# A long convolution by FFT with a maxout MLP behind it: the spectral stage in 32x64 and 64x32 tiles, with the complex product made whole

## The chip, the cores and the metric

The kernel runs on one core of a Trainium2 chip. The metric is the device time of one execution in microseconds, lower is better. Three executions of the kernel before took 496.3, 496.51 and 496.91 us; the median is 496.51. Engines go by the names of the profile: PE is TensorE (matmuls), PEld its weight loads, DVE VectorE, ACT ScalarE, POOL GpSimd, SP SyncE, which only issues DMAs.

## The reference

```python
# x (8, 3072, 256), filt_r and filt_i (1537, 256), all float32
X = np.fft.rfft(x, axis=1)
Y = X * (filt_r + 1j * filt_i)[None]
y = np.fft.irfft(Y, n=3072, axis=1)
# the 8*3072 rows of y as tokens; w1, w2 (256, 1024), w_out (1024, 256)
out = np.maximum(y @ w1, y @ w2) @ w_out          # (24576, 256) float32
```

Each of eight batches is filtered along its 3072 positions in the frequency domain, and every position then goes through a two-branch maxout MLP.

## The kernel before

**The MLP.** Since max(a, b) = max(a - b, 0) + b, the kernel computes relu(y (w1 - w2)) w_out + y (w2 w_out). Wd is w1 - w2, Wo is w_out, and M is w2 w_out, made once. A batch's 3072 tokens are eight tiles of 384. For a tile tt, `moe_h` makes eight hidden blocks: ph, 128 hidden units by 384 tokens, is two matmuls (L483), and is evicted through a relu into gt by DVE (L485) or ACT (L487). `moe_o` of tile tt - 1 runs between them: each block of 128 tokens takes ten matmuls of 256 columns into po (two with M, L535, eight with Wo, L537); two blocks share a bank, DVE evicts them to ot (L548), and `out_block` issues the output DMAs (L496), on POOL's queue for all but the last two tiles.

**The step grid.** The order of the work is written out by hand. The last loop of the kernel goes over tiles tt and j = 0 to 7; a batch is 64 steps, step = 8 (tt mod 8) + j. One step is ph of (tt, j), then three or four po matmuls of tile tt - 1. The FFT of the coming batches is slipped into steps: the table `mid` holds calls made right behind ph, ahead of the po matmuls; `group` holds `s4g` calls made behind the first two po matmuls; `todo` (filled by `plan`) holds calls at a step's end. Each engine takes its instructions in this program order.

**The filter** of a batch has four matmul stages; n runs over parts of the 24 frequency groups, s and g over halves.

- The load and fold: `load_xf` brings a quarter of a half batch from memory (SP), `fold` adds and subtracts the two halves of the sequence on POOL (L104, L105) into xb, in bf16. c = 0 to 7 are the eight quads of a batch.
- S1, `s1`: a quad is four matmuls of 512 columns into two banks, pa0 and pa1, in 64x64 tiles (64 rows of contraction, 64 output columns; four of them cover the 128x128 array). ACT evicts them to `at` (L359), SP writes `ad` in DRAM, and `s1_read` brings it back with the axes turned, as bt.
- S2, `s2`: eight 64x64 matmuls of 256 columns into px0 and px1 (L385). For a frequency group they give the real and the imaginary part of X in different rows.
- The product, `product` on DVE (L391): px times the filter F, both parts of the filter at once, 1024 elements a row, to bf16 pq. It makes the partial products only: X_r F_r, X_r F_i, X_i F_r, X_i F_i.
- S3, `s3`: 16 matmuls of 64x64 and 256 columns into pz0 and pz1 (L409), with the tables VP and VQ. They take the partial products and so do the sums of the complex product in the contraction, along with the first step of the inverse transform. ACT evicts to zt (L413), SP writes `zd` in DRAM, and `z_read` brings it back as zr.
- S4, `s4g`: 16 matmuls of 48 rows for each tile (L444) into pc0, pc1, then ACT (L449) and two DVE operations (L451) give the tokens y of two or three tiles.

`visit(b, n, quads)` puts S3 of part n - 1, S2 of part n, S1 of the listed quads of the batch after it, and the product of part n behind one ph. There are seven visits in a batch, n = 0 to 6, called right behind ph (`mid`), at steps 14, 18, 23, 31, 34 (or 35), 39 and 47 in the batches 2 and later of the grid, a step or so later in batch 1. `s4g` stands at steps 61 (of the batch before), 6 and 27. Batch 0, and the filter of batch 1 within it, go by code of their own (`s1t`, `t1`, `s3t`, `t2`, `f1`, `s4`).

**PSUM.** The pool `ps` has six banks, one for each of ph, pa0, pa1, px0, px1, pz0, pz1, pc and so on; `pso` has two, for po. A tile gets the bank whose last tile was given back first, and its first matmul waits for the engine that reads that one.

ACT_TOO (L475) lists steps at which ACT takes a relu that DVE would take otherwise: from batch 1 on, DVE has 19 of a batch's 64 relus.

## Time and profile before

| | |
|---|---|
| median of three executions | 496.51 us |
| the profiled execution: its own time, and its span | 496.87 us, 495.1 us |
| mean granted clock of TensorE | 0.993 of full speed |
| time between the s4g calls at step 61 of two batches (212.56 to 269.23) | 56.67 us |
| matmuls and weight loads, by the page | 5759 each |
| DMA queue of SP: packets, MB | 64178, 66.71 |
| DMA queue of POOL: packets, MB | 13200, 29.60 |
| HBM read, written | 53.87 MB, 47.19 MB |

The profiled execution is one run under the hardware profiler; the span goes from its first instruction to its last. The page gives busy time by engine, the chain of work that ended last, and the costliest groups of instructions with the idle time ahead of them and what ended it. The views of the trace used below are tables of busy time in chosen stretches, the waits of an engine with what ended them, single lines of the kernel with their durations, and the timeline: start, length, engine, line, operation, what is written from what, how many in a row. Matmuls overlap: one starts before the end of the one ahead of it, so the time of a matmul is read from start to start.

### The profile page before, as it was taken

The numbers are of one execution on the slowest core, as the hardware profiler recorded it, in microseconds if no ns is written. First come the engines' busy times: TensorE is split into PE (matmuls) and PEld (weight loads), VectorE is DVE, ScalarE is ACT, GpSimd is POOL, SyncE is SP. The second block draws the span as 40 slices with busy tenths as digits, with TensorE's granted clock in tenths as the row PEclk, the third lists the DMA queues.
The fourth block names the chain that finished last, engine by engine and source line by source line (L and its number), as shares of the span: only waits on it lengthen the run. The fifth ranks groups of instructions, "written<-read, shape, count | busy, mean of one in ns | idle before, by whom it ended". The sixth has DMA issues, their size and how long they took to land.

```text
span 495.1 us, 14211 instructions
## 1 busy us (share of the span) xinstructions
PE 483.3 (98%) x5759; PEld 353.0 (71%) x5759; DVE 335.5 (68%) x535; ACT 320.3 (65%) x667; POOL 259.7 (52%) x342
## 2 busy tenths in 40 slices
PE   7689999999999999999999999999999999999997
PEld 3457777777777777777777777777777777777775
DVE  7786788467855788458865688458874688556542
ACT  5776478666765677566866677666766656465442
POOL 8795869436368574556637575475642212222220
PEclk9889999999999999999999999999999999999999
DMA  7989998995899786896888966895777435531112
GB/s 120 163 241 229 264 243 258 279 254 167 232 264 250 175 240 194 259 241 186 214 250 234 228 200 201 267 251 166 214 228 190 127 124 152 155 122 66 64 65 86
DMA packets 77587, 97.31 MB, mean 197 GB/s; under 512 B 8945, under 2 KB 55314, under 8 KB 76146
## 3 DMA queue, kind: packets, MB, share of 16 engines
q1 hardware_dynamic: 64178, 66.71, 50.0%
q0 software_dynamic: 13200, 29.60, 21.6%
q8 instruction: 45, 0.74, 0.7%
q14 instruction: 20, 0.16, 0.1%
q10 hardware_dynamic: 144, 0.09, 0.1%
HBM read 53.87 MB, written 47.19 MB: 204 GB/s over the span
## 4 chain that ended last, share of the span: by engine, by line
PE 94%; ACT 2%; DMA 2%; POOL 1%; issue 0%; DVE 0%; POOLq 0%
PE po L537 35%; PE ph L483 34%; PE po L535 9%; PE pz L409 5%; PE pc L444 3%; PE pa L355 2%; PE px L385 2%; DMA xb<-in_x_dram 2%; PE pr L609 1%; PE pt L588 1%; POOL xb L89 1%; PE pa L330 1%; PE py L461 1%; PE pt L582 0%; ACT bt L574 0%
## 5 line engine op out<-in xcount | busy, mean ns | idle before, releaser
L487 ACT ACTIVATE gt<-ph 128x384 bf16<-128x384 f32 x357 | 175.6, 496 | 137.6 <-PE ph L483 134.5
L537 PE MATMUL po<-Wo,gt 128*128 128x256 bf16 x1528 | 262.6, 273 | 0.0
L496 POOL DMA_DIRECT2D out_dram<-ot x186 | 102.9, 556 | 195.5 <-DVE ot L548 179.9
L537 PEld LDWEIGHTS <-gt 128*128 128x128 bf16 x1528 | 144.7, 98 | 66.7 <-issue 12.0
L391 DVE TENSOR_TENSOR pq<-px,F 128x1024 bf16<-128x1024 f32 x91 | 106.9, 1218 | 26.4 <-PE px L385 25.4
L485 DVE TENSOR_SCALAR gt<-ph 128x384 bf16<-128x384 f32 x155 | 83.7, 551 | 52.2 <-PE ph L483 45.9
L483 PEld LDWEIGHTS <-Wd 128*128 128x128 bf16 x1024 | 99.4, 98 | 14.0 <-POOL Wd L298 0.7
L548 DVE TENSOR_SCALAR ot<-po 128x512 f32<-128x512 f32 x83 | 57.0, 686 | 35.0 <-PE po L537 33.1
L104 POOL TENSOR_TENSOR xb<-XF 128x512 bf16<-128x512 f32 x48 | 61.3, 1276 | 23.6 <-DMA XF<-in_x_dram 10.4
L105 POOL TENSOR_TENSOR xb<-XF 128x512 bf16<-128x512 f32 x48 | 61.1, 1272 | 0.0
L359 ACT ACTIVATE at<-pa 128x512 bf16<-128x512 f32 x96 | 51.8, 613 | 3.4 <-PE pa L355 3.3
L413 ACT ACTIVATE zt<-pz 128x512 bf16<-128x512 f32 x84 | 45.6, 594 | 5.7 <-PE pz L409 1.9
L449 ACT ACTIVATE ce<-pc 128x384 f32<-128x384 f32 x56 | 23.7, 491 | 6.3 <-PE pc L444 5.5
L409 PE MATMUL pz<-pq,VP 64*64 64x256 bf16 x336 | 22.2, 281 | 0.0
L385 PE MATMUL px<-bt,U 64*64 64x256 bf16 x384 | 20.2, 280 | 1.2 <-ACT VQ L279 0.7
L409 PE MATMUL pz<-pq,VQ 64*64 64x256 bf16 x336 | 21.1, 269 | 0.0
L409 PEld LDWEIGHTS <-VP 64*64 64x64 bf16 x336 | 10.0, 105 | 13.3 <-issue 12.7
L355 PE MATMUL pa<-xb,CT 64*64 64x512 bf16 x192 | 18.0, 377 | 0.0
L444 PEld LDWEIGHTS <-zr 48*128 48x128 bf16 x896 | 12.9, 93 | 4.4 <-issue 4.4
L444 PE MATMUL pc<-G,zr 48*128 48x48 bf16 x896 | 15.1, 180 | 0.0
L385 PEld LDWEIGHTS <-U 64*64 64x64 bf16 x384 | 10.6, 108 | 3.9 <-issue 3.6
L619 PE MATMUL pd<-W 128*128 128x512 bf16 x28 | 9.6, 456 | 1.5 <-DVE zero L150 1.5
(383 smaller groups left out, 632.0 us busy)
## 6 DMA issues: line engine op xcount, KB each, us to landing
out_dram<-ot POOLq DMA_DIRECT2D x186, 128.0 KB, 3.7
XF<-in_x_dram SPq DMA_DIRECT2D x96, 192.0 KB
ad<-at SPq DMA_DIRECT2D x56, 192.0 KB
zd<-zt SPq DMA_DIRECT2D x42, 256.0 KB
zr<-zd SPq DMA_DIRECT2D x56, 192.0 KB
bt<-ad SPq DMA_DIRECT2D x72, 128.0 KB
WS<-in_moe_w_dram SPq DMA_DIRECT2D x4, 512.0 KB
xb<-in_x_dram POOLq DMA_DIRECT2D x8, 192.0 KB, 6.6
```

The source lines that it names most:

```text
L104: G.tensor_tensor(t_[:, 0], f[:, 0], f[:, 1], OP.add)
L105: G.tensor_tensor(t_[:, 1], f[:, 0], f[:, 1], OP.subtract)
L359: S.activation(at[:, m0:m0 + 2], pa[g], AF.Copy)
L391: E.tensor_tensor(pq, px.rearrange("p (o i) d -> p o i d", o=1).to_broadcast([128, 2, 2, D]), F[:, :, 2 * v:2 * v + 2, s], OP.mult)
L409: TE.matmul(pz[g][64 * s:64 * s + 64, i], tab[64 * g:64 * g + 64, 2 * v + i, s], pq[s][64 * g:64 * g + 64, q, i], start=(q == 0), stop=(q ...
L413: S.activation(zt[:, :, g], pz[g], AF.Copy)
L483: TE.matmul(ph, Wd[:, dc, 128 * j:128 * j + 128], y_[:, dc], start=(dc == 0), stop=(dc == 1))
L485: V.tensor_scalar(gt[tt][:, j], ph, 0.0, None, OP.max)
L487: S.activation(gt[tt][:, j], ph, AF.Relu)
L496: E.dma_start(out=dst, in_=ot[tt // 2][:, 3 * (tt % 2) + c])
L537: TE.matmul(p_, g_[:, n - 2, blk], Wo[:, n - 2], start=(e == 0), stop=(e == 9))
L548: V.tensor_scalar(ot[tt // 2][:, e - 1:e + 1], po[q // 2 % 2], SCALE, None, OP.mult)
```

## The change

The filter of batches 2 to 7 goes another way; batch 0 and batch 1 keep theirs.

1. **S2 in pairs, 64x32 tiles** (`s2_pairs`): sixteen matmuls for eight. The rows of px now hold, for four frequency groups of 32 rows, the real part in one half of the columns and the imaginary part in the other. It needs a table UN, a negative copy of a part of U.
2. **The complex product whole.** `product_pairs` makes the four partial products of n = 0 to 4 on DVE in fp32, as before 1024 elements a row (a small extra operation at n = 0 for one frequency); three steps later `add_pairs` subtracts and adds them on POOL, four operations of 256 elements a row, into one bf16 tile ri. For n = 5 `whole_product` does all of it on DVE: for each half s two multiplications of 512 elements a row, one of them in place in PSUM, and two sums of 256.
3. **S3 once, 32x64 tiles** (`s3_pairs`): 32 matmuls of 32 rows for two parts n at once, into four banks pz0 to pz3, where before the two parts took 32 matmuls of 64 rows. The evictions stay four for two parts; at the third of the three calls of a batch DVE takes two of them.
4. **S1 in 64x32 tiles** for batches 3 and later: eight matmuls of 512 columns a quad for four.
5. **A new plan.** `group_of` puts S3, then the first quad of S1, then S2 and its product, then the other quads behind the first two po matmuls of a step, where `s4g` stands too. Groups at steps 9, 14, 20, 30, 34, 38, 44; `s4g` at 61, 4 and 25. The z reads come in thirds (`z_read3`); loads, folds and the `s1_read` calls have new steps.
6. **Tables.** `to_pairs`, at steps 54, 56 and 60 of batch 0: the copies for UN, fN, VQ, and four DMAs inside F that bring the filter into the order of pairs.
7. **Other places.** From tile 8 on every second output DMA goes by SP's queue. VS gives the steps at which DVE takes the relu: again 19 of 64, in the last batch 24. pqpool has four buffers for six, pq0 eight for six, and w2b and w2T lie in the pool of the fp32 products (`pfpool`, three buffers).

The core of the diff, with the new functions (whole, but for the lists of pools):

```diff
+        if b == 2:
             for g, r in ((0, 0), (1, 1), (0, 1), (1, 0)):
                 TE.matmul(pa[g][64 * r:64 * r + 64], CT[64 * g:64 * g + 64, r], xb[b, c][64 * g:64 * g + 64, r], ...)
+        else:
+            for r in range(2):
+                for h in range(2):
+                    for g in range(2):
+                        TE.matmul(pa[g][64 * r + 32 * h:64 * r + 32 * h + 32], CT[64 * g:64 * g + 64, r, 32 * h:32 * h + 32],
+                                  xb[b, c][64 * g:64 * g + 64, r], start=True, stop=True)
...
+    def s2_pairs(b, n):
+        px = [ps.tile([128, 2, D], FP32, tag="ps", name="px%d" % s) for s in range(2)]
+        for k in range(2):
+            for q in range(4):
+                g, r = divmod(q, 2)
+                u = 4 * n + 2 * r + g
+                for s in range(2):
+                    rows = slice(64 * s, 64 * s + 64)
+                    tab = U[rows, u, 32 * (k ^ r):32 * (k ^ r) + 32] if k * r == 0 else UN[rows, n, g]
+                    TE.matmul(px[s][32 * q:32 * q + 32, k], tab, bt[b][rows, u], start=True, stop=True)
+        return px
+    def filt(n, s, c):
+        return F[:, c, 2 * n, s].rearrange("p (o d) -> p o d", o=1).to_broadcast([128, 2, D])
+    def product_pairs(n, px):
+        pf = []
+        for s in range(2):
+            t_ = pfpool.tile([128, 2, 2, D], FP32, tag="pf", name="pf")
+            V.tensor_tensor(t_, px[s].rearrange("p (o k) d -> p o k d", o=1).to_broadcast([128, 2, 2, D]),
+                            F[:, :, 2 * n, s].rearrange("p c (o d) -> p c o d", o=1).to_broadcast([128, 2, 2, D]),
+                            OP.mult)
+            if n == 0 and s == 0:
+                V.tensor_tensor(t_[0:1, 0, 1], px[0][0:1, 1], fN, OP.mult)
+            pf.append(t_)
+        return pf
+    def whole_product(n, px):
+        ri = pqpool.tile([128, 2, 2, D], BF16, tag="pq", name="ri")
+        for s in range(2):
+            t_ = pfpool.tile([128, 2, D], FP32, tag="pf", name="pf")
+            V.tensor_tensor(t_, px[s], filt(n, s, 1), OP.mult)
+            V.tensor_tensor(px[s], px[s], filt(n, s, 0), OP.mult)
+            V.tensor_tensor(ri[:, s, 0], px[s][:, 0], t_[:, 1], OP.subtract)
+            V.tensor_tensor(ri[:, s, 1], px[s][:, 1], t_[:, 0], OP.add)
+        return ri
+    def add_pairs(b, n):
+        ri = pqpool.tile([128, 2, 2, D], BF16, tag="pq", name="ri")
+        for s, t_ in enumerate(pend[b, n]):
+            G.tensor_tensor(ri[:, s, 0], t_[:, 0, 0], t_[:, 1, 1], OP.subtract)
+            G.tensor_tensor(ri[:, s, 1], t_[:, 0, 1], t_[:, 1, 0], OP.add)
+        pend[b, n] = ri
+    def s3_pairs(b, k, ris):
+        if k == 0:
+            zd[b] = dram.tile([NU, 128, D], BF16, tag="zd", name="zd")
+        pz = [ps.tile([128, 2, D], FP32, tag="ps", name="pz%d" % q) for q in range(4)]
+        for i in range(2):
+            for c, tab in enumerate((VP, VQ)):
+                for s in range(2):
+                    for q in range(4):
+                        rows = slice(32 * q, 32 * q + 32)
+                        TE.matmul(pz[q][64 * s:64 * s + 64, i], tab[rows, 4 * k + 2 * i + q % 2, s],
+                                  ris[i][rows, s, c], start=(c == 0), stop=(c == 1))
+        for g in range(2):
+            zt = zpool.tile([128, 2, 2, D], BF16, tag="zt", name="zt")
+            for r in range(2):
+                if k == 2 and g == 1:
+                    V.tensor_copy(zt[:, :, r], pz[2 * g + r])
+                else:
+                    S.activation(zt[:, :, r], pz[2 * g + r], AF.Copy)
+            nc.sync.dma_start(out=zd[b][8 * k:8 * k + 8].rearrange("(i r g) p d -> g p i r d", r=2, g=2)[g], in_=zt)
+    def group_of(b, n, k, quads):
+        if k is not None:
+            s3_pairs(b, k, [pend.pop((b, 2 * k + i)) for i in range(2)])
+        if b + 1 >= B:
+            quads = ()
+        for c in quads[0:1]:
+            s1(b + 1, c)
+        if n is not None:
+            px = s2_pairs(b, n)
+            pend[b, n] = whole_product(n, px) if n == 5 else product_pairs(n, px)
+        for c in quads[1:]:
+            s1(b + 1, c)
...
-    ACT_TOO = ((7, 6), (0, 1), (0, 6), (1, 1), (3, 6))
+    VS = (1, 3, 8, 13, 18, 24, 28, 30, 34, 38, 44, 46, 48, 50, 52, 54, 56, 58, 60)
...
-        E = G if tt < 8 * B - 2 else nc.sync
+        E = G if tt < 8 or (tt < 8 * B - 2 and (3 * tt + c) % 2 == 0) else nc.sync
...
     for b in range(1, B - 1):
+        for st, n, k, quads in ((9, 0, None, (0, 1)), (14, 1, None, (2, 3)), (20, 2, None, (4,)), (30, 3, 0, ()),
+                                (34, 4, None, (5, 6)), (38, 5, 1, ()), (44, None, 2, (7,))):
+            groups[b, st] = (b + 1, n, k, quads)
+            if n is not None and n < 5:
+                plan(b, st + 3, add_pairs, b + 1, n)
+        for k, n in enumerate((37, 46, 48)):
+            plan(b, n, z_read3, b + 1, k)
...
+            elif (b, step) in groups:
+                moe_o(tt - 1, k, k + 2)
+                group_of(*groups[b, step])
+                k, n = k + 2, n - 2
```

## What was predicted

> **What bounds the kernel now.** I read the page first (busy time, then the chain that ended last), then a table of busy time over a whole batch, then PE's own waits, then the timeline around one visit.
>
> ```profile
> span 495.1 us, 14211 instructions
> ...
> PE 483.3 (98%) x5759; PEld 353.0 (71%) x5759; DVE 335.5 (68%) x535; ACT 320.3 (65%) x667; POOL 259.7 (52%) x342
> ...
> PE 94%; ACT 2%; DMA 2%; POOL 1%; issue 0%; DVE 0%; POOLq 0%
> ```
>
> ```profile
> 269.23:325.90 56.67, 56.67 (x674) 41.73 (x674) 38.95 (x60) 38.72 (x82) 33.21 (x41) 1.00 0.83 225
> ```
>
> ```profile
> PE pa L559 <- DMA xb<-in_x_dram: 1.8, 3, 1.3
> ```
>
> The columns of the table are length, PE, PEld, DVE, ACT, POOL, granted clock and DMA share. A batch takes 56.67 us, PE is busy in all of it at full clock, and the waits put down to PE (ten kinds, this the largest, under 8 us in all) lie in the opening stages. So time goes only where PE streams, changes tile shape, or waits less than the tail of a matmul, which "busy" hides. DVE has 18 us free in a batch, ACT 18, POOL 23.
>
> One visit of before (S3, S2, S1 between a ph and the next ph):
>
> ```profile
> 306.89 0.49 PE L483 MATMUL ph<-y__5618,Wd 128*128 128x384 bf16 x2
> 307.31 0.30 PE L409 MATMUL pz<-pq,VP 64*64 64x256 bf16 x4
> 307.44 0.28 PE L409 MATMUL pz<-pq,VQ 64*64 64x256 bf16 x4
> 307.55 0.28 PE L409 MATMUL pz<-pq,VP 64*64 64x256 bf16 x4
> 307.66 0.28 PE L409 MATMUL pz<-pq,VQ 64*64 64x256 bf16 x4
> 307.77 0.39 PE L385 MATMUL px<-bt,U 64*64 64x256 bf16 x8
> 307.99 0.39 PE L355 MATMUL pa<-xb,CT 64*64 64x512 bf16 x4
> 308.30 0.50 PE L537 MATMUL po<-Wo,gt 128*128 128x256 bf16 x3
> 308.68 0.48 PE L483 MATMUL ph<-y__5623,Wd 128*128 128x384 bf16 x2
> 309.00 0.38 PE L535 MATMUL po<-M,y__5618 128*128 128x256 bf16 x2
> 309.22 0.38 PE L537 MATMUL po<-Wo,gt 128*128 128x256 bf16 x2
> 309.44 0.49 PE L483 MATMUL ph<-y__5623,Wd 128*128 128x384 bf16 x2
> ```
>
> ```profile
> 308.03 1.08 ACT L413 ACTIVATE zt<-pz 128x512 bf16<-128x512 f32 x2
> ```
>
> Four 64x64 matmuls of 256 columns run as one round: rounds start 0.11 us apart, 0.13 behind the entry. A visit's S3 is 4 rounds, S2 two, an S1 quad (512 columns) one of 0.22. The two matmuls of a ph stream 0.325 us (a step of ph and four po takes 0.76, from 308.68 to 309.44, and a po of 256 columns 0.109 like a round), so ph ends at 307.21 and the first S3 round starts 0.09 later. From the S1 round at 307.99, 0.22 long, to po at 308.30 is again 0.09. These are the prices of a change of shape.
>
> ```profile
> 226.13 0.49 PE L483 MATMUL ph<-y__4375,Wd 128*128 128x384 bf16 x2
> ...
> 227.56 0.33 PE L483 MATMUL ph<-y__4375,Wd 128*128 128x384 bf16 x1
> ```
>
> From one ph to the next, less 0.325 for ph and 0.109 for each po, that first visit of a batch (S2, S1) costs 0.67 us; the one above 1.79 - 0.325 - 0.327 = 1.14. All seven visits from 226 to 259 us, worked the same way: 0.67, 1.10, 1.10, 1.10, 1.12, 1.14, 1.14, together **7.37 us**. In the last producing batch, without S1, it is 0.45, five of 0.89 and 0.67, together 5.55.
>
> **What the change removes and adds on PE.** S3 goes from 24 rounds in a batch to 12, if eight 32x64 tiles run in a round: 12 x 0.109 = 1.31 us less. S2 and S1 double their instructions (16 and 8 for 8 and 4) in tiles half as wide, the same rounds if eight run at once. No 32-row tile is in the trace; 64x32 is, at the building of the tables:
>
> ```profile
> 20.75:20.79 0.04, 0.03 (x8) 0.03 (x8) 0.04 (x1) 0.04 (x1) 0.04 (x1) 1.00 0.11 15
> 20.79:20.82 0.03, 0.03 (x16) 0.03 (x16) 0.03 (x1) 0.03 (x1) 0.03 (x1) 1.00 0.04 0
> ```
>
> In stretches of 0.032 us the count of matmuls under way grows by 8: eight 64x32 tiles start every 32 ns, so eight in 109 ns is no limit of issue. I take full concurrency for 32x64 too (nearest row); the other end is four at a time. The Trainium skill, "TensorE: Matmul & The Clock Gate", section "Wait — 56ns, not 53.3ns?", says start-to-start never drops below about 25 ns; by that, 18 S3 groups of 32 matmuls would take 0.80 us for 0.44 and 36 S2 of 16 take 0.40 for 0.22, 13 us more and 509 in all. The rows above show 4 ns from start to start, so by them the rule does not hold for tiles side by side, and I give it no chance beyond that of the last rival.
>
> Shape changes: seven entries and exits stay; three groups of a batch now change inside from 32x64 to 64x32, which no row shows; between nothing and the 0.13 us of an entry's first round plus 0.09, I take 0.09 plus 0.02 of slower first round. If nothing else happened, a middle batch's seven groups would cost three at 1.03 (S3 with S2 or S1), three at 0.89 (S1, S2, S1) and one at 0.69: 6.5 us, 0.9 less than 7.37.
>
> **What then is late.** ps has six banks. A group of six takes them all, and in the built program the next ph gets the bank that the group's first tile held (pz0, or pa0). Its eviction must end first. The chain in before:
>
> ```profile
> 400.29 0.28 PE L409 MATMUL pz<-pq,VQ 64*64 64x256 bf16 x4
> ...
> 400.61 1.09 ACT L413 ACTIVATE zt<-pz 128x512 bf16<-128x512 f32 x2
> ```
>
> ```profile
> 170.13 0.39 PE L355 MATMUL pa<-xb,CT 64*64 64x512 bf16 x4
> ...
> 170.56 0.60 ACT L359 ACTIVATE at<-pa 128x512 bf16<-128x512 f32 x1 [0.84 <-PE pa L355]
> ```
>
> ```profile
> L413 ACT ACTIVATE zt<-pz 128x512 bf16<-128x512 f32 x84 | 45.6, 594 | 5.7 <-PE pz L409 1.9
> ```
>
> From the start of the last S3 round, 0.32 us to ACT, 0.594 for pz0, and 0.05 to PE (308.03 + 0.594 = 308.62, ph at 308.68): 0.97. In before S2, S1, the exit and three po cover it to within 0.04 us, which is the difference between 1.10 and 1.14 above. In the changed kernel two of the four po stand ahead of the group and S3 and S1 are seldom together, so less stands behind S3:
>
> - Groups at steps 30, 38 (S3, S2) and 44 (S3, S1). ph ends at 0; two po 0.218, change 0.094, rounds at 0.31, 0.45, 0.555, 0.664. pz0's last matmul is the fifth of eight, with a wait on a weight load ahead of it: 0.03 to 0.04 more. Next ph at 0.664 + 0.04 + 0.97 = 1.67. PE alone would be there at about 1.47. Less four po: **1.235** each instead of 1.03.
> - Groups at 9, 14, 34 (S1, S2, S1). pa0 starts at 0.31, its last matmul 0.04 later; 0.43 to ACT, 0.605, 0.05: next ph at 1.44, PE alone 1.32. Less four po: **1.00** each.
> - Group at 20 has four tiles: no wait, 0.69.
>
> Sum 3.71 + 3.00 + 0.69 = 7.40, against 7.37: +0.03 us a batch, five times. The dearer the inner change of shape, the more of it these waits hide, up to 0.2 us. In the last producing batch there is no S1: four groups at 0.45, two at 1.235, one S3 alone 0.71, sum 4.98 against 5.55: -0.57. **Together 0.15 - 0.57 = -0.4 us**.
>
> The Trainium skill, "TensorEngine Tiling (Array Packing)", section "PSUM Bottleneck", speaks against the change in the same sense: after a speedup by tiling the PSUM copy may become the bottleneck. By that sentence alone all 0.9 us a batch could go; the rows above say how much of it does.
>
> **Work beside PE, costed at nothing.**
>
> ```profile
> L496 POOL DMA_DIRECT2D out_dram<-ot x186 | 102.9, 556 | 195.5 <-DVE ot L548 179.9
> ...
> L391 DVE TENSOR_TENSOR pq<-px,F 128x1024 bf16<-128x1024 f32 x91 | 106.9, 1218 | 26.4 <-PE px L385 25.4
> ...
> L548 DVE TENSOR_SCALAR ot<-po 128x512 f32<-128x512 f32 x83 | 57.0, 686 | 35.0 <-PE po L537 33.1
> ```
>
> ```profile
> L399 POOL TENSOR_TENSOR pq<-xs,F x1: 660/660/660, 32.8 to 32.8; 128x256 bf16<-128x256 f32 x1
> ```
>
> ```profile
> L397 DVE TENSOR_TENSOR pq<-px,F x1: 680/680/680, 32.9 to 32.9; 128x512 bf16<-128x512 f32 x1
> ```
>
> ```profile
> L398 DVE TENSOR_TENSOR pq<-px,F x1: 411/411/411, 33.5 to 33.5; 128x256 bf16<-128x256 f32 x1
> ```
>
> POOL: an add_pairs is four 128x256 operations, 4 x 0.66 = 2.64 us, five in a batch, 13.2; half of the output DMAs leave it (12 x 0.55 = 6.6). 33.2 + 6.6 = 40 of 56.7. In order behind folds, the add of product 3 ends some 5 us after the ph of step 30 (the product 3.7, then half an add), and the S3 of step 38 comes 8.4 after it (1.35 for the rest of group 30, the group at 34, seven steps of 0.65 or 0.76): 3 us of cover, beyond which PE waits for POOL one to one. DVE: ten products of 1.22 (fp32 out is in no row of that shape, but the 128x512 fp32 eviction and the bf16 product differ by 0.01), one small extra (0.41), a whole product and two zt copies (0.68): 38.95 + 3.7 = 42.6. The whole product at step 38 is four operations of 0.68 and four of 0.41, overlapping by 0.08, 4.0 us; it starts 1.36 after ph and ends at 5.4, and S3 of step 44 needs its second half at 6.1: 0.65 us of cover. ACT loses two evictions. SP gains 12 output DMAs and four reads a batch and waits in order for DVE's evictions; behind them stand x loads, used eleven steps later, and the z reads, needed 13 steps (9.5 us) after step 48. The table steps at 54 to 60 are a few small operations and four DMAs, ten steps ahead of use.
>
> **The sum.** The profiled run took 496.87 (span 495.1, 1.8 around it): 496.87 - 0.4 = 496.45. It stands 0.36 above the median of 496.51; on the median's footing **496.1 us**. Differences under 0.2% (1 us: 495.5 to 497.5) are about what a measurement of this kernel cannot tell from no change.
>
> **Rivals.**
>
> 1. The eviction does not hold the next ph. For: the stalls are 0.1 to 0.2 us each, inside a matmul's tail, and the tiles may drain sooner. Against: 1.14-us visits show exactly this wait. Then 0.9 us a batch is won five times, and 1.0 in the last (two groups at 1.03 for 1.235): 5.5 us, 491. Half of it gives 493.5. Chance 0.28 for 491 to 495.
> 2. DVE becomes late at step 44. Beyond 0.65 us of delay, each us holds S3 on PE, in six batches. The in-place multiplications in PSUM and the self-waits of the whole product are in no row. If the two in-place ones take twice 0.68, DVE ends 1.36 later, PE waits 0.7, 4.3 us in all: **500.4**. For: four dependent operations in a row, with an eviction and a relu right behind. Against: DVE stays idle a quarter of the batch. Chance 0.22 for 497.5 to 501.
> 3. The change does not do what it says: 32-row tiles run four at a time. Then each of 18 S3 groups has 0.436 more: 496.1 + 7.8 = 504. Against: the 64x32 rows. Chance 0.08.
>
> The forecast, that waits behind the new groups take back what S3 gives, has 0.42, with its own range 494.8 to 497.5. Of it I put 0.30 within 0.2%, 0.08 below, 0.04 above. So faster 0.28 + 0.08 = 0.36, same 0.30, slower 0.22 + 0.08 + 0.04 = 0.34. The range takes rival 1 to 493.0 and rival 2 to 500.5; outside stay about 0.07 below and 0.11 above.
>
> **What the new profile would show.** Right: S3 rounds of eight starting 0.11 us apart, four to a group; a change inside the group of about 0.1; the ph behind steps 30, 38, 44 starting 0.05 us after the first zt ends, about 1.67 after the ph before; a middle batch of 56.7 us, the last shorter by 0.5. Wrong: PE waiting for POOL or DVE at S3 (rival 2), S3 rounds 0.22 apart (rival 3), or a ph right behind two po with zt still running (rival 1).

## The result: 515.7 us after 496.7, and the profile after the change

The changed kernel took 515.73 us in the median of four runs (514.75 to 517.65), the kernel before 496.71 (496.30 to 497.78) beside it: a ratio of 1.0384, 95% interval 1.035 to 1.0419. It is 19 us slower, outside the range on record. The profiled execution took 517.65 us.

The page of the kernel after: the span, the busy times, the granted clock in 40 slices, the chain that ended last.

```profile
span 515.8 us, 15430 instructions
...
PE 489.7 (95%) x6204; PEld 347.1 (67%) x6207; DVE 359.5 (70%) x597; ACT 308.5 (60%) x651; POOL 297.7 (58%) x381
...
PEclk9889999999998999989999899999999999999999
...
PE 73%; DMA 8%; SPq 5%; issue 4%; POOL 4%; ACT 3%; DVE 1%; POOLq 0%; ACTq 0%; DVEq 0%
PE ph L591 27%; PE po L645 26%; PE po L643 7%; DMA zr<-zd 5%; PE pc L552 3%; SPq L387 3%; PE pa L365 2%; PE pz L501 2%; DMA xb<-in_x_dram 2%; SPq L97 1%; ACT zt L509 1%; PE px L457 1%; POOL xb L107 1%; DMA XF<-in_x_dram 1%; SPq L372 1%
```

PE had 94% of the chain before and has 73 now, and the granted clock shows eights where all was full speed behind the opening. The largest part of what took its place is the z read (zr<-zd): its transfers have 5%, and SP's issue of them at L387 has 3%. The waits of PE and of its weight loads say where it is felt (total us, times, longest):

```profile
PE pc L552 <- DMA zr<-zd: 9.4, 9, 2.4
```

```profile
PEld L552 <- DMA zr<-zd: 6.1, 4, 2.7
```

L552 is `s4g`. Its cost at step 61, worked out like the visits of the prediction (ph to ph, less 0.325 and 0.109 for each po), was 0.83 us before; in four batches it is now 4.07, 4.56, 3.43 and 2.97 us. From 95 us to the last s4g, the s4g calls cost 30.5 us for 16.2, steps without a call 6.1 us for 0.2 (most of it in the steps right behind an s4g), the groups 42.9 for 42.7. So 20.5 of the 20.8 us between the two profiled executions (517.65 and 496.87 us) are found in these steps, and the groups have next to no part in them.

The table of busy time around one such wait (length, PE, PEld, DVE, ACT, POOL, clock, DMA share, GB/s):

```profile
218.00:220.11 2.11, 2.11 (x19) 1.59 (x17) 0.79 (x2) 0.73 (x2) 1.26 (x2) 1.00 0.57 203
220.11:223.25 3.14, 0.71 (x6) 0.30 (x4) 1.01 (x2) 0.49 (x1) 1.95 (x3) 1.00 0.62 230
...
224.00:225.00 1.00, 1.00 (x47) 0.96 (x47) 0.02 (x1) 0.54 (x2) 0.00 (x0) 0.50 0.87 260
225.00:226.00 1.00, 1.00 (x9) 0.59 (x5) 1.00 (x3) 0.71 (x2) 0.00 (x0) 0.50 1.01 250
...
228.00:229.00 1.00, 1.00 (x11) 0.80 (x9) 0.03 (x1) 0.53 (x2) 1.00 (x1) 1.00 0.62 159
```

PE is busy 0.71 of 3.14 us, and right behind that its clock is granted at 0.50. The trace has four such stretches in the middle of the run, one behind each of the four waits, each 3.41 us long: 1.7 us lost each, 6.8 in all. The four waits themselves, worked out from the costs of step 61 and of the steps behind it less that 1.7, are 2.1 to 2.9 us, so with the half clock each costs 1.6 to 1.8 times its length.

SP's queue explains the wait. First before, then after (start, length, line, what, how many DMAs); the second ph matmul of step 61, from which the times below are counted, starts at 212.09 there and 220.27 here:

```profile
202.82 0.38 SPq L414 DMA_DIRECT2D zd<-zt  x1
204.78 0.79 SPq L362 DMA_DIRECT2D ad<-at  x2
205.96 3.66 SPq L377 DMA_DIRECT2D zr<-zd  x4
209.72 0.92 SPq L94 DMA_DIRECT2D XF<-in_x_dram  x2
```

```profile
208.28 3.38 SPq L510 DMA_DIRECT2D zd<-zt  x2
211.76 0.93 SPq L372 DMA_DIRECT2D ad<-at  x2
212.78 0.67 SPq L604 DMA_DIRECT2D out_dram<-ot  x1
213.54 1.88 SPq L97 DMA_DIRECT2D XF<-in_x_dram  x2
215.47 5.66 SPq L387 DMA_DIRECT2D zr<-zd  x8
221.23 0.59 SPq L604 DMA_DIRECT2D out_dram<-ot  x1
```

Before, four reads go out straight behind the S1 write, the last of them done 2.5 us ahead of step 61. After, the second zd write waits for a zt buffer (the 3.38 us hold two DMAs of 0.38), then an S1 write, an output and an x load stand in front, and then come eight reads, the last of them done 0.9 us behind it. The s4g of step 61 uses tokens of m = 0 to 11, so the reads of m = 0 to 15 alone: the first two of four before; the first two and the fifth and sixth of eight after, as `z_read3` goes through both halves of one part before the next.

### The profile page after: what moved, and what is told of

Read it like the earlier page. It is cut to its first block, busy times and chain, and to the rows that moved or that the text cites. A ratio compares the mean times of both kernels' runs of the same rounds, so it can differ in the third digit from the quotient of the medians.

```text
span 515.8 us, 15430 instructions
## 1 busy us (share of the span) xinstructions
PE 489.7 (95%) x6204; PEld 347.1 (67%) x6207; DVE 359.5 (70%) x597; ACT 308.5 (60%) x651; POOL 297.7 (58%) x381
## 3 DMA queue, kind: packets, MB, share of 16 engines
q0 software_dynamic: 9312, 18.98, 14.5%
## 4 chain that ended last, share of the span: by engine, by line
PE 73%; DMA 8%; SPq 5%; issue 4%; POOL 4%; ACT 3%; DVE 1%; POOLq 0%; ACTq 0%; DVEq 0%
PE ph L591 27%; PE po L645 26%; PE po L643 7%; DMA zr<-zd 5%; PE pc L552 3%; SPq L387 3%; PE pa L365 2%; PE pz L501 2%; DMA xb<-in_x_dram 2%; SPq L97 1%; ACT zt L509 1%; PE px L457 1%; POOL xb L107 1%; DMA XF<-in_x_dram 1%; SPq L372 1%
## 5 line engine op out<-in xcount | busy, mean ns | idle before, releaser
L645 PE MATMUL po<-Wo,gt 128*128 128x256 bf16 x1528 | 271.3, 275 | 0.4 <-DVE gt L593 0.4
L604 POOL DMA_DIRECT2D out_dram<-ot x105 | 58.8, 561 | 132.0 <-DVE ot L656 108.4
L467 DVE TENSOR_TENSOR pf<-px,F 128x1024 f32<-128x1024 f32 x60 | 71.2, 1217 | 18.9 <-PE px L457 7.0
L656 DVE TENSOR_SCALAR ot<-po 128x512 f32<-128x512 f32 x83 | 56.9, 685 | 16.6 <-PE po L645 16.0
L488 POOL TENSOR_TENSOR ri<-pf 128x256 bf16<-128x256 f32 x60 | 43.5, 725 | 13.3 <-DVE pf L467 13.1
L489 POOL TENSOR_TENSOR ri<-pf 128x256 bf16<-128x256 f32 x60 | 43.3, 721 | 0.0
L509 ACT ACTIVATE zt<-pz 128x512 bf16<-128x512 f32 x60 | 31.3, 601 | 18.4 <-PE pz L501 18.4
L552 PE MATMUL pc<-G,zr 48*128 48x48 bf16 x896 | 17.1, 183 | 10.9 <-DMA zr<-zd 9.4
L552 PEld LDWEIGHTS <-zr 48*128 48x128 bf16 x896 | 14.2, 95 | 16.4 <-issue 8.5
L410 DVE TENSOR_TENSOR pq<-px,F 128x1024 bf16<-128x1024 f32 x19 | 22.1, 1216 | 2.5 <-PE px L404 2.2
L365 PE MATMUL pa<-xb,CT 64*32 64x512 bf16 x320 | 17.5, 385 | 0.1
L457 PE MATMUL px<-bt,U 64*32 64x256 bf16 x432 | 14.7, 273 | 0.4 <-ACT at L369 0.4
L507 DVE CAST zt<-pz 128x512 bf16<-128x512 f32 x12 | 7.7, 685 | 6.1 <-DMA zd<-zt 4.2
L479 DVE TENSOR_TENSOR pf<-px,F 128x512 f32<-128x512 f32 x12 | 8.2, 686 | 4.0 <-POOL ri L489 2.6
```

The lines of the kernel that those rows point to most:

```text
L467: V.tensor_tensor(t_, px[s].rearrange("p (o k) d -> p o k d", o=1).to_broadcast([128, 2, 2, D]), F[:, :, 2 * n, s].rearrange("p c (o d) -> ...
L488: G.tensor_tensor(ri[:, s, 0], t_[:, 0, 0], t_[:, 1, 1], OP.subtract)
L552: TE.matmul(pc[s][k][:, dc, m], zr[b][64 * s:64 * s + 48, 4 * i + m, 128 * dc:128 * dc + 128], G2[64 * s:64 * s + 48], start=True, stop=True)
L604: E.dma_start(out=dst, in_=ot[tt // 2][:, 3 * (tt % 2) + c])
L645: TE.matmul(p_, g_[:, n - 2, blk], Wo[:, n - 2], start=(e == 0), stop=(e == 9))
L656: V.tensor_scalar(ot[tt // 2][:, e - 1:e + 1], po[q // 2 % 2], SCALE, None, OP.mult)
```

## The experiments

Each was timed beside the kernel before on the same chip. The ratios are to that, with their 95% intervals. A run that has no other start named is the changed kernel with the edit shown.

### Is it the queue ahead of the reads?

Three theories say what makes the reads late. Theory A: the outputs that now go by SP. Theory B: the wait of the zd write for one of three zt buffers. Theory C: eight reads in one stretch. One edit for each, then all three at once (`three`):

```diff
-        E = G if tt < 8 or (tt < 8 * B - 2 and (3 * tt + c) % 2 == 0) else nc.sync   # outs_pool
+        E = G if tt < 8 * B - 2 else nc.sync
-    zpool = ctx.enter_context(tc.tile_pool(name="zpool", bufs=3))                   # zt4
+    zpool = ctx.enter_context(tc.tile_pool(name="zpool", bufs=4))
-        for k, n in enumerate((37, 46, 48)):                                        # zr43
+        for k, n in enumerate((37, 43, 48)):
```

> The changed kernel with all output DMAs back on POOL's queue (but for the last two tiles, as before). Start: 515.7 us against 496.7 before; in four batches PE stands 2.1 to 3.7 us too long at the s4g of step 61, waiting for the z reads, and each time the granted clock then is 0.50 for 3.4 us, 1.7 us more. Theory A, the outputs on SP's queue are what makes the z reads late: the waits at step 61 fall under 1 us, no stretch at half clock, time 497 to 503. Theory B, the third zt buffer: DVE's zt at step 44 still waits about 1.5 us or more for a zd write to land, the reads still come late, time 508 to 515. Theory C, eight z reads in one stretch on SP behind that zd write (5.6 us of issue): the reads start only about 0.8 us earlier (one output less ahead of them), time 510 to 515.

519.45 us, ratio 1.0444 (1.0402 to 1.0487): slower still, where A allowed 503 at most. A fell.

> The changed kernel with four zt buffers for three (UN lies in W1's place to make room). Theory B: DVE's zt at step 44 no longer waits, the second zd write goes out 1.9 us earlier, the reads end 1.9 us earlier, the waits at step 61 fall from 2.1-3.7 to 0.2-1.8 us and most stretches at half clock go: time 500 to 507. Theory A (outputs on SP) and theory C (eight reads in one stretch): the wait moves to the next item of SP's queue, the gain is under 1 us a batch, 511 to 516.

516.65 us, 1.0388 (1.0352 to 1.0424): no gain. B fell, and this run says why. SP's queue in it (step 61 at 219.03):

```profile
207.58 0.93 SPq L510 DMA_DIRECT2D zd<-zt  x2
208.60 1.52 SPq L372 DMA_DIRECT2D ad<-at  x2
210.22 0.80 SPq L604 DMA_DIRECT2D out_dram<-ot  x1
211.11 1.34 SPq L96 DMA_DIRECT2D XF<-in_x_dram  x2
212.51 5.66 SPq L387 DMA_DIRECT2D zr<-zd  x8
```

The wait for the buffer is gone and SP begins to issue the reads 6.5 us ahead of step 61 instead of 4.8. But in the trace's packet records the packets of the S1 write and the x load run until 215, and only then do those of the reads (8 KB each) get going, 14 to 19 in a us until 221. Their last one ends at 223.55, 4.5 us behind step 61, where it was 4.6. The queue is full of bytes issued earlier; issuing sooner only puts the reads into that line sooner.

> The changed kernel with the second third of the z reads (four DMAs) issued at step 43 instead of 46, so ahead of the zd writes of step 44 on SP's queue. Theory C: 2.8 us of issue leave the stretch behind the last zd write; the waits at step 61 fall by as much, to under 1 us, the half clock goes, 498 to 503. Theory B: DVE's zt still waits for the zt buffer, and SP now also waits for the landing of the zd writes of step 38, so little is won, 509 to 516. Theory A: outputs still stand between, 508 to 515.

513.68 us, 1.0328 (1.0291 to 1.0366): at most 2 us gained, since this interval touches that of the changed kernel. That is far from C's 498 to 503 and within the ranges of A and B. SP now waits for the landing of the second part's zd writes ahead of these reads (11.2 us in eight waits, a row that the changed kernel does not have), and the third part's zd writes stand behind them.

> All three at once: outputs on POOL, four zt buffers, second third of the z reads at step 43. If the z reads are the whole loss: no wait at step 61, no stretch at half clock, a middle batch of 56.7 us as the PE sum of the prediction has it, 495.5 to 498. If something else is lost as well (plain steps slower, x loads late for POOL's folds), 499 to 508.

524.25 us, 1.0532 (1.0495 to 1.0568): the slowest so far, with a stretch at half clock behind step 61 in six batches and 1.5 us more at step 38 of batch 1. None of the three theories is the cause by itself, nor are the three together; why the three edits are worse than each alone stays open.

### Are the reads themselves too slow?

In the packet records seldom more than eight of the z reads' 8 KB packets are under way at once after the change (39% of the time exactly eight), and seldom more than twelve before it. Theory E: a third of z has eight frequency groups, a half twelve, and that sets how many transfer engines work. The Trainium skill, "DMA: Bandwidth & Descriptors", section "Why a DMA increments its semaphore by 16 and not by 1", says that a DMA uses the largest number up to 16 that divides the slowest dimension of both sides. The trace agrees: eight, twelve, and six in before_six below. Theory F: SP's issue, 0.65 us for each read, is the limit. Theory D: the bytes that stand ahead in the queue are the limit.

```diff
-        zd[b] = dram.tile([NU, 128, D], ...)          # zlay; zlay32 reads all 32 m in one DMA as well
+        zd[b] = dram.tile([2, NU, 2, NM, D], ...)
...
-        src = zd[b][8 * k:8 * k + 8].rearrange("u (s r m) d -> s u r m d", s=2, r=2)
+        src = zd[b][s, 8 * k:8 * k + 8].rearrange("u q m d -> (u q) m d")
```

> The changed kernel with zd laid out as halves s first, so that the 16 rows of a z read lie at one stride in memory (the twelve z reads as before; a zd write becomes two of 64 rows). In the traces so far at most eight packets of 8 KB are under way at once after the change and twelve before it. Theory E, eight transfer engines for a third of z instead of twelve for a half: a read of 128 KB takes two packets of 0.44 us on each engine, 0.88 us, as long as 192 KB took before, and eight in a row 7.0 us; here sixteen packets will be under way, eight reads are bound by SP's 0.70 us each, 5.6 us, two more writes cost 0.8 us of SP, so the waits at step 61 fall by 0.5 to 1.5 us and the time to 507 to 514. Theory F, SP's 0.65 us of issue for each read is the limit, not the transfers: nothing is gained and two writes are added, 515 to 520. Theory D, too many bytes on the way at once: no gain, 514 to 518.

523.86 us, 1.0526 (1.0488 to 1.0564). Up to sixteen packets are under way now, but one takes 0.59 us instead of 0.44, and the two more writes stand ahead of the reads. This run cannot tell the two apart.

> The layout of the kernel above, and a third of z read in two DMAs of 256 KB instead of four of 128 KB. Theory E: sixteen transfer engines, 256 KB in 0.88 us, the four DMAs behind the last zd write 3.5 us instead of 7.0; less 0.8 us for the two writes, the waits at step 61 fall by 2 to 3 us, to under 1 us, the stretches at half clock go, 497 to 505. Theory F alone: SP issues half as many reads, the same gain, but then at most eight or so packets under way. Theory D: the bytes are the same, no gain, 512 to 518.

545.49 us, 1.0961 (1.0905 to 1.1016). A packet is now 16 KB and takes 1.56 us, 3.6 times as long as one of 8 KB. E is right about the number of engines and wrong as a remedy.

```diff
-                plan(b, (-30 if first else -33) + 7 * c, load_xf, b + 2, c)                      # after_x
+                plan(b, (-30 if first else -33) + 7 * c + (5 if c == 2 else 0), load_xf, b + 2, c)
-                plan(b, (-24 if first and c < 2 else -23 if first else -22) + 7 * c, fold, b + 2, c)
+                plan(b, (-24 if first and c < 2 else -23 if first else -22) + 7 * c + (4 if c == 2 else 0), fold, b + 2, c)
```

> The changed kernel with the x load of step 45 (two DMAs, 384 KB, 1.9 us of SP) moved behind the z reads, to step 50, and its fold from 56 to 60. Theory D, the bytes ahead of the last z reads: the reads start 1.9 us earlier, the waits at step 61 fall to 0.2 to 1.8 us, time 503 to 509. Theory E: the reads start earlier too but drain at eight engines; in the run with four zt buffers they were issued 3 us earlier and landed no more than 1 us earlier, so a gain of 0 to 1 us a batch, 510 to 516.

506.30 us, 1.0173 (1.0127 to 1.0219): 9.4 us won by moving two DMAs of the 16 x loads of a batch, and the fold that needs them, to later steps. This is D's number, not E's: what stands in SP's queue ahead of the reads decides. (The expectation has the reads of `zt4` 3 us earlier, by the clock of the trace; counted from step 61 it is 1.7.)

```diff
+        w = 6 if b >= 2 and h == 1 else 12            # before_six, in z_read of the kernel before
+        for u in range(12 * h, 12 * h + 12, w):
```

> The kernel before with the second half of z read in eight DMAs of six frequency groups instead of four of twelve, at the same step, from batch 2 on: the same bytes, and by theory E six transfer engines for twelve. Theory E: six packets under way, 0.88 us for each 96 KB, 7.0 us for 3.5; with about 1 us to spare at step 61 PE waits some 2.5 us a batch in six batches, and where that brings the clock to half, 1.7 us more: 508 to 522. Theory D (bytes): no difference, 496 to 498. Theory F (issue by SP, 0.65 to 0.75 us each, 5.6 us for 3.7): about 1 us of wait, 499 to 505.

516.51 us, 1.0378 (1.03 to 1.0456): the kernel before, with its z reads alone cut finer, loses as much as the whole change. E, F or both can make this; D alone cannot.

### Is it the order of the reads?

Theory G joins these: reads that step 61 does not need, and loads, stand ahead of those that it needs.

```diff
-        for k, n in enumerate((37, 46, 48)):
-            plan(b, n, z_read3, b + 1, k)
+        for k, n, ms in ((0, 37, (0, 16)), (1, 46, (0,)), (2, 48, (0,)), (1, 50, (16,)), (2, 51, (16,))):
+            plan(b, n, z_read3, b + 1, k, ms)         # z_read3 then loops over ms
```

> The changed kernel with only the order of the z reads altered: for the second and third parts first the halves m = 0 to 15, which the s4g of step 61 uses, then m = 16 to 31 (steps 50 and 51), which the s4g of step 4 and 25 use. Theory G, the z reads that step 61 needs stand too far back in SP's order: two reads of the second part no longer stand ahead, 1.4 us of issue or 1.8 us of transfer, so the waits of 0.7 to 2.5 us ahead of the s4g fall to 0 to 0.7, the stretches at half clock go, 500 to 506. Theory D, too many bytes in all: the same bytes, a gain of under 2 us, 513 to 517.

501.24 us, 1.0081 (1.0053 to 1.0108). The order of eight DMAs, four of which are thereby issued three or four steps later, gives 14.5 of the 19 us back. SP's queue (step 61 at 214.37), and what is left of the waits:

```profile
206.49 1.17 SPq L97 DMA_DIRECT2D XF<-in_x_dram  x2
207.72 2.88 SPq L387 DMA_DIRECT2D zr<-zd  x4
210.69 0.60 SPq L604 DMA_DIRECT2D out_dram<-ot  x1
211.34 2.75 SPq L387 DMA_DIRECT2D zr<-zd  x4
```

```profile
PEld L552 <- DMA zr<-zd: 0.7, 3, 0.2
```

The four reads that step 61 needs have been issued 3.8 us ahead of it, the s4g there costs at most 1.20 us, and no stretch at half clock is left in the middle of the trace. The opposite in the kernel before:

```diff
+        if b >= 2 and h == 1:                         # before_rev, in z_read of the kernel before
+            ms = (16, 0)
```

> The kernel before with the four reads of the second half of z in the other order, m = 16 to 31 first, from batch 2 on: the same DMAs, bytes and steps. In its own trace the last packet of these reads ends 0.5 to 0.9 us after the ph of step 61, and the s4g stands 0.48 behind that ph with no wait, as it uses the first two reads alone. Theory G (the reads that step 61 needs, and where they stand in SP's order, decide): s4g then waits for the last of them, 0.4 to 1 us in six batches, no window of the clock lost: 498.5 to 503. If the slack at step 61 is larger than that, or s4g waits for all four anyway: 496.5 to 497.5, no difference.

507.35 us, 1.0204 (1.0182 to 1.0226): 10.6 us lost by turning four DMAs round, in the direction of G, but outside its 498.5 to 503. The s4g costs 1.3 to 3.4 us for 0.83, so a wait is 0.4 to 2.5 us where 0.4 to 1 was allowed, and one stretch at half clock follows, where none was. The expectation had the last packet of these reads end 0.5 to 0.9 us behind the ph of step 61; in the trace of the kernel before it is 0.5 to 1.4 us in five of six batches. That explains a part of the longer waits, and the rest stays open. PE's waits there:

```profile
PE pc L446 <- DMA zr<-zd: 7.0, 8, 1.7
```

So the kernel before stood on the same edge, with its reads in the right order.

> The changed kernel with the z reads ordered as in the run with the first halves first (501.2 us), and all outputs back on POOL's queue. Theory G: with that order step 61 has about 1.5 us to spare, so 12 outputs more or less on SP decide nothing there, 499 to 503. If outputs on POOL hurt by themselves, as in the run with outputs on POOL alone (519.5 against 515.7: POOL's folds and adds stand behind them, and a stall of 1.5 us at step 38 in batch 1 came up), 502 to 506.

505.38 us, 1.0172 (1.0154 to 1.019). From batch 2 on step 61 has no more waits than with the outputs on SP, as G has it, and the middle batches are as long; what is lost lies in batch 1 (61.5 us for 58.7), most of it on POOL's side: step 38 costs 2.75 us for 1.24 and step 25 2.11 for 1.28, while DVE waits for POOL's adds. Another 0.6 us is at step 61 of that batch. Half of the outputs on SP is the better place.

### Where is the rest?

xm: the ordered reads and the x load of step 45 at step 51. xmz: four zt buffers too. xmz_po1: moreover `moe_o(tt - 1, k, k + 1)` for `k + 2` ahead of `group_of`.

> The order of the reads as above, and the x load of step 45 at step 51 (its fold at 60). Theory G: no wait at step 61 in any batch, none at half clock; what remains of the loss is batch 1 (1.1 us at step 14 and 1.5 us at step 25, seen in every variant so far), so 496.5 to 500. Were something else lost beside PE's waits at s4g, 500 to 506.

502.30 us, 1.0106 (1.0083 to 1.0129). Middle batches of 56.97 us (one 57.19), none waiting at step 61, as G has it; but the time is above its 496.5 to 500, and no better than that of `m_first`. Batch 1 took 59.4 us for 56.9 before.

> The kernel above with four zt buffers. Theory G: nothing waits at step 61 there, so an earlier zd write brings nothing, within 1 us of it. If waits of some batch are left above, they shrink by up to 1.8 us each.

500.59 us, 1.0069 (1.0049 to 1.0088): 1.7 us better, where 1 was allowed; the middle batches are the same 56.97. In the two traces the gain lies ahead of the first step 61 (97.5 us for 99.6), where the traces of all these kernels spread from 97.5 to 100.8; so nothing here shows that the buffer won it. One of the middle batches:

```profile
215.15:272.11 56.96, 56.72 (x753) 40.08 (x753) 42.60 (x69) 36.86 (x80) 40.12 (x48) 1.00 0.79 220
```

Against 56.67 before, 0.30 us is left in it, all in one place: the second ph behind the s4g of step 4 starts 0.30 late, in every batch. Its weight load waits for DVE's tokens of the first tile:

```profile
166.16 0.11 PEld L591 LDWEIGHTS <-Wd 128*128 128x128 bf16 x2 [0.41 <-DVE y__3548 L559]
```

So it seems to lie in the bank that DVE reads there. Before, and behind the s4g of step 61, the same ph has no such wait. In the changed kernel itself, with the s4g at step 4 as well and DVE at the same place, it has it in batch 1 alone.

> The kernel above with each group behind one po of its step instead of two, so three po stand between a group and the next ph. By the prediction's step on evictions, the next ph waits for the eviction of the group's first tile in six of a middle batch's seven groups (1.235 and 1.00 us); each po moved behind the group takes 0.109 us of such a wait away: 1.13 and 0.89, 0.65 us a batch, 3.5 us in all, 493 to 496.5. If the eviction does not hold the ph (rival 1), no gain: the same as the kernel above. If the sixth tile of a group then waits for the relu of the ph ahead of it, up to 0.1 us a group is given back.

499.65 us, 1.0057 (1.0036 to 1.0077), above the 493 to 496.5 expected. A group with S3 and S2, with one po ahead of it:

```profile
245.18 0.49 PE L591 MATMUL ph<-y__4757,Wd 128*128 128x384 bf16 x2
...
246.06 0.29 PE L501 MATMUL pz<-ri,VQ 32*64 32x256 bf16 x8
...
246.66 0.50 PE L645 MATMUL po<-Wo,gt 128*128 128x256 bf16 x3
247.07 0.32 PE L591 MATMUL ph<-y__4757,Wd 128*128 128x384 bf16 x1
```

From ph to ph 1.89 us against 2.00, so 1.13 for 1.24: the 0.109 of one po, as the eviction wait has it. Of the groups with S1 three got dearer instead (1.04 and 1.05 us at steps 9 and 34 for 1.00, 1.29 at step 44 for 1.24): the matmuls into their last tile start 0.04 to 0.05 us behind the end of the relu of the ph just ahead, as they would if it lay in that bank. The gain nets to 0.08 us a batch.

The last three kernels take xmz, one po ahead of the groups with S3 and S2 only, and later folds in batch 1; the s4g of step 4 stands at 6, 5 and 4.

```diff
+                h = 1 if groups[b, step][2] is not None and groups[b, step][1] is not None else 2
...
-                plan(b, (-24 if first and c < 2 else -23 if first else -22) + 7 * c, fold, b + 2, c)
+                plan(b, ... + 7 * c + (4 if c == 2 else 6 if first and c > 4 else 0), fold, b + 2, c)
...
-        group[b, 4] = range(t + 3, t + 6)
+        group[b, 6] = range(t + 3, t + 6)
```

> All that the runs point to: order of the z reads, x load of step 45 behind them, four zt buffers (500.6 us together); one po instead of two ahead of the groups with S3 and S2 alone (1.24 to 1.13 us measured, twice a batch, 1.3 us in all); in batch 1 the folds of the last three quads six steps later, behind the adds that DVE's products wait for there (part of 3.1 us); s4g of step 4 at step 6 as in the kernel before, for the 0.30 us by which the step behind it is late in every batch now (2.1 us). 494.5 to 497.5 if all hold; 497 to 500 if the later s4g collides with DVE's product at step 9.

504.60 us, 1.0152 (1.0139 to 1.0166), above both ranges: the later s4g collides with the group at step 9, which costs 1.95 us for 1.00. Nor did the late ph go: with the s4g at step 6, as in the kernel before, the second ph behind it is 0.40 us late, by the same wait.

```profile
226.30 0.11 PEld L591 LDWEIGHTS <-Wd 128*128 128x128 bf16 x2 [0.52 <-DVE y__4775 L559]
```

> The kernel above with that s4g at step 5 instead of 6. If DVE's product at step 9 holds the one at 6, this is the better, 494.5 to 497.5; if not, the same or up to 2 us slower.

500.39 us, 1.0086 (1.0055 to 1.0117): 4 us better than that, and above the 494.5 to 497.5 hoped for. The group at step 9 costs 1.31 and the 0.30 stays.

> The kernel with the s4g at step 5 (500.4 us), with that s4g back at step 4. There DVE's operations for the tokens end before the product of step 9: the group at step 9 should cost 1.00 us again instead of 1.31 (0.31 in each of six batches, 1.9 us), while the step behind the s4g stays 0.30 us late. By the sum of PE's gaps: 497.5 to 499, level with the kernel before but for the 2.1 us of those late steps; batch 1 without its stall at step 25. Above 500, the sum over PE's gaps misses something.

499.33 us, 1.0039 (1.0022 to 1.0057), a little above the 497.5 to 499 expected: the best variant of the changed kernel, and 0.4% behind the kernel before. Its middle batches take 56.75 us against 56.67, the 0.30 included. So none of the runs beat the kernel before. The gap behind the opening is now batch 1: 59.7 us for 56.9. POOL and DVE there, in xmz:

```profile
114.05 1.26 POOL L106 TENSOR_TENSOR xb<-XF 128x512 bf16<-128x512 f32 x1 [3.71 <-DMA XF<-in_x_dram]
115.28 1.27 POOL L107 TENSOR_TENSOR xb<-XF 128x512 bf16<-128x512 f32 x1
116.50 1.11 POOL L604 DMA_DIRECT2D out_dram<-ot  x2
117.63 0.74 POOL L488 TENSOR_TENSOR ri<-pf 128x256 bf16<-128x256 f32 x1
```

```profile
119.08 1.23 DVE L467 TENSOR_TENSOR pf<-px,F 128x1024 f32<-128x1024 f32 x1 [2.60 <-POOL ri L489]
```

A fold waits 3.7 us for its x load; behind it on POOL stands the add of product 0; DVE waits for its fp32 buffer to write the next product; and the bank of px comes free late, for the s4g of step 25. Later folds removed that stall (2.07 us at step 25 for 0.61), but in best4 steps 20 and 38 then cost 0.9 and 1.0 us more; in best5 they did not, and batch 1 took 58.1. In every variant step 14 of batch 1 costs 2.06 us for 1.00. In `xmz` its S2 waits there 0.3 us for the read of bt and then 0.4 us for ACT's eviction of pa; what makes these late stays open.

## Why the prediction was wrong, point by point

**Rounds and shapes: right.** A group with S3 and S2 of the kernel after:

```profile
253.90 0.49 PE L591 MATMUL ph<-y__4758,Wd 128*128 128x384 bf16 x2
254.22 0.38 PE L645 MATMUL po<-Wo,gt 128*128 128x256 bf16 x2
254.54 0.32 PE L501 MATMUL pz<-ri,VP 32*64 32x256 bf16 x8
254.67 0.29 PE L501 MATMUL pz<-ri,VQ 32*64 32x256 bf16 x8
254.78 0.29 PE L501 MATMUL pz<-ri,VP 32*64 32x256 bf16 x8
254.89 0.29 PE L501 MATMUL pz<-ri,VQ 32*64 32x256 bf16 x8
255.11 0.39 PE L457 MATMUL px<-bt,U 64*32 64x256 bf16 x10
...
255.45 0.39 PE L645 MATMUL po<-Wo,gt 128*128 128x256 bf16 x2
255.90 0.49 PE L591 MATMUL ph<-y__4758,Wd 128*128 128x384 bf16 x2
```

Eight 32x64 tiles at once, rounds 0.11 apart, four to a group; 0.11 more at the inner change (254.89 + 0.11 to 255.11). Rival 3 fell.

**The ph waits for pz0's eviction: right.** ACT's evictions of that group:

```profile
255.25 2.06 ACT L509 ACTIVATE zt<-pz 128x512 bf16<-128x512 f32 x4 [1.10 <-PE pz L501]
```

255.25 + 0.60 + 0.05 is the 255.90 above, 2.00 from ph to ph as worked out (1.67 + 0.325). The seven groups of a middle batch cost 1.00, 1.00, 0.665, 1.24, 1.00, 1.24, 1.24, in sum 7.37 for 7.40 predicted and 7.37 before; the last producing batch 4.96 for 4.98. Rival 1 fell, in the trace and by xmz_po1. What S3 wins on PE goes into these waits.

**DVE and POOL: right in the middle batches.** The whole product took 4.08 us for 4.0, and step 44 never waited for it, although it began 1.74 us behind the ph for 1.36, which left about 0.3 of the 0.65 us of cover: rival 2 fell. An operation of the adds took 0.72 us for 0.66. Batch 1 had no sum of its own in the prediction. There a fold that waits for its load stands ahead of the adds, DVE waits for them, and s4g at step 25 for DVE: 0.9 us (1.5 in other variants), by a path that the prediction does not have. The 3 us of cover ahead of step 38 held in the changed kernel; with all outputs on POOL they did not (1.5 us at step 38 of batch 1).

**SP: this is the step that failed.** The prediction counted 12 outputs and four reads more on SP, named the z reads as needed "13 steps (9.5 us) after step 48", and costed all of it at nothing. With the reads in order the outputs cost little there (`m_first` and `m_first_outs` differ by at most 0.3 us at step 61 from batch 2 on). But the 9.5 us were counted from the step at which the reads are planned. Steps 46 and 48 end at 209.34 and 210.75; SP gets to their reads at 215.47 and 218.39, 6 and 7.6 us later, behind the zd writes, the S1 write, an output and the x load. Then the eight need 5.7 us of issue and about 7 of transfer (8 x 2 packets of 0.44 us on an engine), and the last two that step 61 needs stand fifth and sixth. In place of nothing, PE waits 2.1 to 2.9 us at step 61 in four batches. `m_first` and `after_x` show that this is the failed step: with the reads in order of use 14.5 us come back, and with one x load out of their way 9.4. The same sum for the kernel before would have shown its edge: the last read issued 2.5 us ahead of step 61, its last packet ending 0.5 to 1.4 us behind it in five of six batches.

**The clock** was in no term: each of the four waits cost 1.7 us more by the half clock behind it.

**The moved s4g** (step 6 to 4) was costed at nothing, and in the changed kernel that is nearly so: the step behind it is late by 0.29 us in batch 1 alone. In the variants with the reads in order it is 0.30 us in each of seven batches, 2.1 us, but the step is not the cause: at step 6 it is 0.40 (`best6`). What put that ph behind DVE's tokens stays open.

With the order mended and one x load moved (`xm`), the middle batch is 56.97 us where 56.70 was predicted, and the difference is about the 0.30 of this ph. Most of what then remains is batch 1, 2.5 us.

## What to carry to other kernels

Where DMAs are issued in order, as by SP here, the time of a read is not its step but the sum of issue and transfer of all that stands ahead of it; work that sum out for the last read that each consumer needs, and issue first what is used first. A wait on the busiest engine that just fits shows nothing in a profile: compare the landing of each transfer with its use before you thicken its queue. And a new order of steps should be summed for the first batch too, where other loads are on the way.

## What the runs showed of the hardware that was not expected

- **The clock falls after far less than a whole idle window.** In every trace the half-clock stretches begin on a grid of 3.413 us and last one to three of its windows, unless the trace ends first. Behind the first 40 us of the 19 traces, a window at full clock in which PE stood idle for 1.532 us or more (after: 1.53, 2.20, 2.61, 2.70) had half clock in the next one, even when the idle time was in two pieces (1.12 and 0.58 us in after_x); those with 1.530 us (before_six) or less did not. Idle is here what the profile's modelled ends of matmuls leave. So the same wait may cost 1.7 us more or nothing, by where it lies: in before_six a wait of 2.8 us split between two windows (1.34 and 1.47) lowered no clock. The Trainium skill, "TensorE: Matmul & The Clock Gate", section "Part 1: The HAM clock gate (the "warmup" mystery)", has a free-running window of about 3.4 us, and this trace agrees; that an idle window is needed for the clock to fall does not hold here.
- **More engines gave less than in proportion, and larger packets gave nothing.** A packet of 8 KB of the z reads took 0.44 us with up to eight under way (after), 0.47 with up to twelve (before) and 0.59 with up to sixteen (zlay): with all of them busy that is 149, 210 and 222 GB/s, an estimate from these times. A packet of 16 KB took 1.56 us with up to sixteen (zlay32), 168 GB/s. Other transfers ran beside them in each trace.
